# Three tiles per width transform, a smaller first weight load and a shorter warm-up memset in a fused spectral and GELU kernel

**Chip, cores, metric.** One NeuronCore of one Trainium2 chip. The metric is device microseconds of one execution. An execution's time is about 2.1 us more than the span that its trace covers.

## What is computed

The reference adds three terms for an input x of 2048 rows and 640 columns (bf16):

```
xn  = layernorm(x)                                # per row
A   = irfft2(rfft2(xn) * (w_r + 1j*w_i))          # 2-D transform over 2048 x 640, filter, back
B   = gelu(xn @ w1 + b1) @ w2 + b2               # w1: 640 x 1536, w2: 1536 x 640
out = x + A + B
```

Both transforms are written as matrix products with small tables of cosines and sines. A "tile" below is one of the 16 groups of 128 rows.

## The kernel before

The kernel is a list of operations, each with an engine, a priority and an estimate of its length. A list scheduler in the file orders them per engine and sets the semaphores. So any setting (priorities, zones of PSUM banks, which tiles are staged) acts through the resulting order. PSUM is the memory that TensorE writes its products to. TensorE's work in order of time: a warm-up on constants; products with W1 (128 columns for tiles 0 and 1, then 256 and 512), into which transposes and the transforms are woven; products with W2; final products.

The settings, the loads of the head and the warm-up:

```python
STAGED = (0, 2, 4, 6, 8, 10)      # tiles whose W2 product is finished early and parked in SBUF
LAG = 4                           # by how many tiles VectorE's folding trails its normalisation
WARM = 10
...
load_x(0, 1)
...                               # identity, b1
load_x(1, 1)
load_w1(0)                        # each part: three chunks of 128 columns, 480 KB
load_w1(1)
load_w1(2)
load_x(2, 2)                      # tiles 2 and 3
load_w1(3)
...
K.op([("dve", 0.3)], 200, ... e.memset(gT[:, 0, 0:640], 0.5), writes=[B_wm])
warm = K.op([("pe", WARM * 0.43)], 200, mms(lambda: [(ps(B_wp.slot, 0, 512),
            gT[:, 0, 0:128], gT[:, 0, 128:640], True, True)] * WARM), ...)
```

The width transform of two tiles, once along D before the filter (table `etab`) and once after it (`getab`). 640 columns are folded to four sums of 160 terms; of these, 128 rows are the main product, and the remaining 32 rows of all four sums run side by side on four strips of 32 rows:

```python
def five(bufs, main, rem, tab):
    lst = []
    for n, part in ((0, 0), (0, 1), (1, 1), (1, 0)):      # tile, main (0) or remainder (1)
        for g in range(4):
            o_ = ps(bufs[g // 2].slot + g % 2, Q4 * n, Q4 * n + Q4)
            if part == 0:
                lst.append((o_, main(g, n), tab[:, Q4 * g:Q4 * g + Q4], n == 0, n == 1))
            else:
                lst.append((o_, rem(g, n), tab[32 * g:32 * g + 32, 4 * Q4:5 * Q4], n == 1, n == 0))
    return lst
```

The order main 0, remainder 0, remainder 1, main 1 means that TensorE leaves the 128-row form once per pair of tiles. I call that an excursion. Eight pairs along D and eight after the filter make 16.

Of the kernel before, what the change touches and what calls it, by code (L numbers as in the profile page):

```python
# [8 lines left out]
F32 = dt.float32  # L9
# [4 lines left out]
D = 640  # L14
F = 1536
H2 = 320
# [98 lines left out]
ZONE = {'hps': ((2, 8), (0, 4), (2, 8), (2, 8), (0, 4), (4, 8), (2, 8)), 'bps': (0, 4), 'cps': (0, 8), 'dps': (0, 4), 'eps': (0, 6), 'fps': (2, 8), 'fst': (0, 8), 'yps': (0, 8), 'tps': (2, 6), 'aps': (0, 8)}  # L115
PRIO = {'hps': 41.9, 'gelu': 211.2, 'pb': 57.3, 'pc': 141.2, 'filt': 203.4, 'ipc': 358.6, 'xb': 326.2, 'eps': 56.7, 'fin': 29.1, 'fst': 17.0}
BLOCKS = ((0, 1), (1, 2), (2, 4), (4, 6), (6, 8), (8, 12), (12, 16))
AHEAD = 3
STAGED = (0, 2, 4, 6, 8, 10)
XRAT = 4  # L120
LAG = 4
WARM = 10
DEPTH = 5
PACE = 5
BYDMA = (6, 7, 8, 9, 10, 11, 12, 13, 14, 15)

# [266 lines left out]
def bass_parallel_sum__spectral_gfnet__dense_activation_gelu__prompt_kernel(  # L393
# [21 lines left out]
    with ExitStack() as es:  # L415
# [23 lines left out]
        W1 = sb("W1", [128, 4, 5, 384])  # L439
# [5 lines left out]
        xb4 = sb("Xb", [128, 2, 4 * KP])  # L445
# [5 lines left out]
        xot = sb("xo", [128, 5, D], F32)  # L451
# [6 lines left out]
        YO, Y2, YF = 0, 6 * D, 10 * D  # L458
# [9 lines left out]
        p_xn, p_x1, p_xf, p_xb, p_y, p_t, p_z, p_zs = Pool(4), Pool(2), Pool(2), Pool(2), Pool(2), Pool(2), Pool(2), Pool(2)  # L468
        p_yo, p_y2, p_yf, p_xo, p_os = Pool(3), Pool(2), Pool(3), Pool(5), Pool(4)
# [23 lines left out]
        K.op([("pool", 0.1)], 99, lambda e, _: e.memset(view(xb4, KP - 2, [[2 * KP, 4], [1, 3]]), 0.0), writes=[B_xbpad])  # L493
        K.op([("pool", 0.1)], 99, lambda e, _: e.memset(view(xb4, 2 * KP - 1, [[2 * KP, 4], [1, 1]]), 0.0), writes=[B_xbpad])
# [5 lines left out]
        B_w1s = [Buf(f"w1_{j}") for j in range(4)]  # L500
# [8 lines left out]
        def load_w1(j):  # L509
            load(W1[:, j, :, :], w1v[:, :, 384 * j:384 * j + 384], B_w1s[j], 491520, rate=340e3)  # L510
# [36 lines left out]
        K.op([("dve", 0.3)], 200, lambda e, _: e.memset(gT[:, 0, 0:640], 0.5), writes=[B_wm])  # L547
        warm = K.op([("pe", WARM * 0.43)], 200, mms(lambda: [(ps(B_wp.slot, 0, 512), gT[:, 0, 0:128], gT[:, 0, 128:640], True, True)] * WARM), reads=[B_wm], writes=[B_wp])

# [98 lines left out]
        for blk, (c0, c1) in enumerate(BLOCKS):  # L648
            s0, s1 = 128 * c0, 128 * c1
            for fc in range(NFC):  # L650
                hps = Buf(f"hps{blk}_{fc}", psum, 1, ZONE["hps"][min(blk, len(ZONE["hps"]) - 1)])
                B_gT[blk, fc] = Buf(f"gT{blk}_{fc}")
                pr = PRIO["hps"] - blk - fc / 20
                part = []
                for js in ((0, 1, 2), (3, 4)):
                    part = [K.op([("pe", len(js) * mm_us(s1 - s0))], pr + 0.01 * len(part), mms(lambda s0=s0, s1=s1, fc=fc, hps=hps, js=js: [
                        (ps(hps.slot, 0, s1 - s0), W1[:, fc // 3, j, 128 * (fc % 3):128 * (fc % 3) + 128], xnT[:, j, s0:s1], j == 0, j == 4) for j in js]),
                        reads=[B_w1s[fc // 3]] + B_xnT[c0:c1], writes=[hps], gate=part)]
                hps_ops.setdefault(blk, []).append(part[0])
                K.op([("act", act_us(s1 - s0, 1))], pr + PRIO["gelu"], lambda e, _, s0=s0, s1=s1, fc=fc, hps=hps: e.activation(  # L660
                    gT[:, fc, s0:s1], ps(hps.slot, 0, s1 - s0), ACT.Gelu_apprx_tanh, bias=b1col[:, fc:fc + 1], scale=1.0),
                    reads=[hps, B_b1c], writes=[B_gT[blk, fc]], after=())
# [3 lines left out]
        def five(bufs, main, rem, tab):  # L666


            lst = []
            for n, part in ((0, 0), (0, 1), (1, 1), (1, 0)):  # L670
                for g in range(4):
                    o_ = ps(bufs[g // 2].slot + g % 2, Q4 * n, Q4 * n + Q4)
                    if part == 0:
                        lst.append((o_, main(g, n), tab[:, Q4 * g:Q4 * g + Q4], n == 0, n == 1))
                    else:
                        lst.append((o_, rem(g, n), tab[32 * g:32 * g + 32, 4 * Q4:5 * Q4], n == 1, n == 0))
            return lst

        def two(buf):
            return PS[buf.slot // 2][:, :].rearrange("p (b n) -> p b n", b=2)[:, :, 0:2 * Q4].rearrange("p b (n k) -> p n b k", n=2)  # L680
        IPC = 0.78
        FIVE = 1.0
        pb_ops, filt_ops, cps_ops, t_ops = [], [], {}, {}
        B_v = [Buf(f"v{q}") for q in range(16)]
        for pair in range(8):
            Y, TB, Z, xb = Buf(f"Y{pair}", p_y), Buf(f"T{pair}", p_t), Buf(f"Z{pair}", p_z), Buf(f"xb{pair}", p_xb)
            bps = [Buf(f"bps{pair}_{v}", psum, 2, ZONE["bps"]) for v in range(2)]
            pb_ops.append(K.op([("pe", FIVE)], PRIO["pb"] - pair / 5, mms(lambda pair=pair, bps=bps: five(
                bps, lambda g, n: Xa[:, g, 2 * pair + n, :], lambda g, n: Xa[32 * g:32 * g + 32, 4, 2 * pair + n, :], etab)),
                reads=B_xa + [B_e], writes=bps, gate=cps_ops.get(pair - 2, [])))  # L690
            for v in range(2):
                K.op([("dve", dve_us(640)), ("act", act_us(640))], PRIO["pb"] - pair / 5,
                     copy(lambda v=v, xb=xb: view(xb4, xb.slot * 4 * KP + v * (KP + 1), [[2 * KP, 2], [1, 2], [2, Q4]]),
                          lambda v=v, bps=bps: two(bps[v])), reads=[bps[v]], writes=[xb])
            cps = [Buf(f"cps{pair}_{r}", psum, 2, ZONE["cps"]) for r in range(2)]
            cps_ops[pair] = [K.op([("pe", 0.78)], PRIO["pc"] - pair / 5, mms(lambda pair=pair, cps=cps, xb=xb: [
                (ps(cps[r].slot + hi, 0, KP)[64 * qq:64 * qq + 64], mtab[64 * hi:64 * hi + 64, 1 if pair == qq == 0 else 0, v, r, :],
                 xb4[64 * hi:64 * hi + 64, xb.slot, (2 * qq + v) * KP:(2 * qq + v + 1) * KP], v == 0, v == 1)
                for r in range(2) for v in range(2) for hi in range(2) for qq in range(2)]), reads=[xb, B_xbpad, B_m], writes=cps, gate=t_ops.get(pair - 2, []))]
# [66 lines left out]
        B_w2s = [Buf(f"w2_{i}") for i in range(4)]  # L766
        for i in range(4):
            load(W2[:, 3 * i:3 * i + 3, :], w2v[:, 3 * i:3 * i + 3, :], B_w2s[i], 491520, after=[o for blk in hps_ops for o in hps_ops[blk][3 * i:3 * i + 3]])
# [14 lines left out]
        def second(c, pcs, fps, gate, done):  # L783

            part = list(gate)
            for f0 in range(0, NFC, 2):
# [3 lines left out]
                    reads=B_w2s[f0 // 3:(f0 + 1) // 3 + 1] + [B_gT[block_of[c], fc] for fc in range(f0, f0 + 2)], writes=[fps], gate=part)]  # L790
# [9 lines left out]
        for cp in range(8):  # L800
            yo, y2, yf = Buf(f"yo{cp}", p_yo), Buf(f"y2{cp}", p_y2), Buf(f"yf{cp}", p_yf)
            pr = PRIO["eps"] - cp / 5
            eps_ = [Buf(f"eps{cp}_{v}", psum, 2, ZONE["eps"]) for v in range(2)]
            K.op([("pe", FIVE)], pr, mms(lambda cp=cp, eps_=eps_: five(
                eps_, lambda g, n: V[:, (0, 2, 3, 1)[g], 2 * cp + n, :], lambda g, n: V[32 * g:32 * g + 32, 4, 2 * cp + n, :], getab)),
                reads=B_v + [B_ge], writes=eps_, gate=[fin_ops[2 * cp - 5]] if cp > 2 else [])
            for v in range(2):
                K.op([("act", act_us(640)), ("dve", dve_us(640))], pr,
                     copy(lambda v=v, yo=yo: view(Wf, YO + yo.slot * 2 * D + H2 * v, [[D, 2], [Q4, 2], [1, Q4]]),
                          lambda v=v, eps_=eps_: two(eps_[v])), reads=[eps_[v]], writes=[yo], after=filt_ops)  # L810
            for k, op in enumerate((ALU.add, ALU.subtract)):
                K.op([("dve", dve_us(D, 2))], pr + 2, lambda e, _, k=k, op=op, yo=yo, y2=y2: e.tensor_tensor(  # L812
                    out=view(Wf, Y2 + y2.slot * 2 * D + (H2 - 1) * k, [[H2, 4], [1 - 2 * k, Q4]]),
                    in0=view(Wf, YO + yo.slot * 2 * D, [[H2, 4], [1, Q4]]), in1=view(Wf, YO + yo.slot * 2 * D + Q4, [[H2, 4], [1, Q4]]), op=op),
                    port=True, reads=[yo], writes=[y2])
            for k, op in enumerate((ALU.add, ALU.subtract)):
                K.op([("dve", dve_us(D, 2))], pr + 3, lambda e, _, k=k, op=op, y2=y2, yf=yf: e.tensor_tensor(
                    out=view(Wf, YF + yf.slot * 2 * D + (D - 1) * k, [[D, 2], [1 - 2 * k, H2]]),
                    in0=view(Wf, Y2 + y2.slot * 2 * D, [[D, 2], [1, H2]]), in1=view(Wf, Y2 + y2.slot * 2 * D + H2, [[D, 2], [1, H2]]), op=op),
                    port=True, reads=[y2], writes=[yf])  # L820
            for n in range(2):
                c = 2 * cp + n
# [10 lines left out]
                for pcs in (WHOLE,) if c < 15 else (((0, 0, H2),), ((0, H2, H2 + Q4),), ((0, H2 + Q4, D),)):  # L833
                    a, b = pcs[0][1], pcs[-1][2]
                    os_, fps = Buf(f"os{c}_{a}", p_os), Buf(f"fps{c}_{a}", psum, len(pcs), ZONE["yps" if c in STAGED else "fps"])
                    if c not in STAGED:
                        part = second(c, pcs, fps, part + fin_gate(c), False)
                    fin_ops[c] = K.op([("pe", sum(mm_us(hi - lo) for _, lo, hi in pcs))], PRIO["fin"] + 1 - c / 10, mms(lambda c=c, n=n, pcs=pcs, yf=yf, fps=fps: [
                        (ps(fps.slot + k, 0, hi - lo), htab[:, c, :], view(Wf, YF + yf.slot * 2 * D + D * n + lo, [[1, hi - lo]]), c in STAGED, True) for k, lo, hi in pcs]),
# [38 lines left out]
```

## Time and profile before

| | before |
|---|---|
| time, median of the first three executions | 154.83 us (154.74 to 154.84) |
| span of the profiled execution | 154.2 us |
| time of that same execution | 156.34 us |
| TensorE busy | 149.2 us, 97% |

The lines of the profile are shown and read in the prediction. Two hints for reading them: a timeline row is a merged run of equal instructions, so the distance from the start of one row to the start of the next is what the engine spent; the length of a matmul (219 to 380 ns) is its latency, not its cost: 128-column products of 219 ns start every 56 ns at full clock.

### The profile page before, as it was taken

The page shows a single profiled execution, that of the slowest core. Times are in us where ns is not written, and L with a number is a line of the kernel's source. Part 1 is how long each engine was busy: PE and PEld are TensorE (multiplying, and loading weights), DVE is VectorE, ACT ScalarE, POOL GpSimd, SP SyncE. Part 2 cuts the span into 40 slices and gives each one's busy share as a digit, 9 for nine tenths or more (in the row PEclk, how much of TensorE's full clock was granted, in tenths as well). Part 3 has the DMA queues.
Part 4 walks back from the last instruction along what each step waited for, and adds up shares of the span by engine and source line. Part 5 has one row for each costly group of instructions (what it writes and reads, how often), then busy time and mean ns, then how long its engine had stood idle before and what let it go on. Part 6 is the DMA issues. An engine that isn't in the chain of part 4 may idle for free.

```text
span 154.2 us, 3759 instructions
## 1 busy us (share of the span) xinstructions
PE 149.2 (97%) x1546; PEld 103.4 (67%) x1546; DVE 117.1 (76%) x267; ACT 86.8 (56%) x176; POOL 21.0 (14%) x33
## 2 busy tenths in 40 slices
PE   5899999999999999999999999999999999999993
PEld 2399888899665536445556766766777777777773
DVE  3859699999994799499499769768977988862222
ACT  3169978998796697878877536873303333210000
POOL 1201120111200000000000022493022221020000
PEclk9999999999999999999999999999999999999999
DMA  4999934869989300134214043199956346541111
GB/s 115 314 367 397 267 100 91 248 139 121 166 168 201 116 0 0 17 115 132 59 70 132 0 89 76 31 222 253 228 128 168 98 123 173 129 128 47 45 71 56
DMA packets 20792, 20.81 MB, mean 135 GB/s; under 512 B 8360, under 2 KB 17448, under 8 KB 20648
## 3 DMA queue, kind: packets, MB, share of 16 engines
q1 hardware_dynamic: 18304, 15.30, 38.1%
q0 software_dynamic: 2304, 5.24, 15.1%
q8 instruction: 12, 0.20, 0.5%
q10 hardware_dynamic: 168, 0.04, 0.1%
q14 instruction: 4, 0.03, 0.1%
HBM read 13.69 MB, written 2.62 MB: 106 GB/s over the span
## 4 chain that ended last, share of the span: by engine, by line
PE 92%; DMA 4%; ACT 1%; DVE 1%; SPq 1%; issue 0%
PE ps L477 91%; DMA W<-in_B_w_dram 4%; PE ps L602 1%; ACT Xb L484 1%; SPq L472 1%; DVE xnT L487 0%; DVE ost L842 0%
## 5 line engine op out<-in xcount | busy, mean ns | idle before, releaser
L477 PE MATMUL ps<-xnT,W 128*128 128x256 bf16 (+2 forms) x420 | 58.2, 294 | 0.9 <-DMA W<-in_B_w_dram 0.6
L477 PE MATMUL ps<-W,gT 128*128 128x320 bf16 (+1 forms) x396 | 56.5, 295 | 0.0
L477 PEld LDWEIGHTS ps<-W,gT 128*128 128x128 bf16 x396 | 37.4, 98 | 14.3 <-issue 0.8
L477 PEld LDWEIGHTS ps<-xnT,W 128*128 128x128 bf16 x420 | 36.1, 101 | 14.3 <-issue 1.3
L660 ACT ACTIVATE gT<-ps,b1col 128x256 bf16<-128x256 f32 (+2 forms) x84 | 40.3, 506 | 8.8 <-PE ps L477 6.2
L842 DVE TENSOR_TENSOR ost<-ps,xo 128x640 bf16<-128x640 f32 (+2 forms) x12 | 8.6, 713 | 12.4 <-PE ps L477 12.4
L829 ACT ACTIVATE xo<-b2bc 128x640 f32<-128x640 bf16 x10 | 7.1, 731 | 19.1 <-DVE ost L842 19.1
L574 DVE BATCH_NORM_STATS2 stats<-XV 128x6 f32<-128x320 bf16 x32 | 14.1, 469 | 2.1 <-DMA XV<-in_A_x_dram 2.0
L831 POOL DMA_DIRECT2D xnT<-in_A_x_dram x6 | 5.4, 900 | 61.1 <-DVE xnT L798 61.1
L716 DVE TENSOR_TENSOR T<-Y,Wf 128x1288 bf16<-128x1288 bf16 x16 | 12.6, 829 | 0.8 <-ACT Y L484 0.2
L831 POOL DMA_DIRECT2D xo<-in_A_x_dram x10 | 9.5, 1043 | 18.7 <-ACT xo L829 18.7
L582 POOL TENSOR_TENSOR rstd<-ve,mhalf 128x2 f32<-128x2 f32 (+1 forms) x9 | 6.3, 703 | 34.7 <-DVE ve L581 34.7
L484 ACT ACTIVATE Xb<-ps 128x640 bf16<-128x640 f32 x9 | 7.9, 895 | 3.7 <-PE ps L477 3.7
L487 DVE CAST Y<-ps 128x644 bf16<-128x644 f32 x8 | 6.6, 828 | 4.3 <-PE ps L477 4.1
L484 ACT ACTIVATE XV<-ps 128x640 bf16<-128x640 f32 x11 | 7.4, 700 | 4.0 <-PE ps L477 3.9
L484 ACT ACTIVATE Wf<-ps 128x640 bf16<-128x640 f32 x10 | 6.7, 694 | 4.0 <-PE ps L477 4.0
L477 PE MATMUL ps<-etab,XW 128*128 128x160 bf16 (+1 forms) x128 | 8.6, 233 | 0.0
L477 PE MATMUL ps<-getab,XV 128*128 128x160 bf16 (+1 forms) x128 | 8.6, 233 | 0.0
L812 DVE TENSOR_TENSOR Wf<-Wf 128x640 bf16<-128x640 bf16 x16 | 7.1, 485 | 1.3 <-ACT Wf L484 1.3
L477 PEld LDWEIGHTS ps<-etab,XW 128*128 128x128 bf16 (+1 forms) x128 | 5.5, 95 | 3.8 <-DVE Y L487 0.7
L487 DVE CAST Xb<-ps 128x640 bf16<-128x640 f32 x7 | 6.2, 885 | 2.2 <-PE ps L477 2.2
L484 ACT ACTIVATE XW<-ps 128x640 bf16<-128x640 f32 x11 | 7.4, 700 | 0.5 <-PE ps L477 0.5
(49 smaller groups left out, 146.4 us busy)
## 6 DMA issues: line engine op xcount, KB each, us to landing
W<-in_B_w_dram SPq DMA_DIRECT2D x8, 480.0 KB, 4.7
xo<-in_A_x_dram POOLq DMA_DIRECT2D x10, 320.0 KB, 4.9
out_dram<-ost SPq DMA_DIRECT2D x15, 160.0 KB, 2.3
XV<-in_A_x_dram SPq DMA_DIRECT2D x7, 320.0 KB, 8.0
xnT<-in_A_x_dram POOLq DMA_DIRECT2D x6, 320.0 KB, 4.6
Wf<-in_A_w_r_dram SPq DMA_DIRECT2D x7, 160.5 KB, 4.8
Wf<-in_A_w_i_dram SPq DMA_DIRECT2D x7, 160.5 KB, 3.8
gtab<-c_G SPq DMA_DIRECT2D x1, 512.0 KB, 7.3
```

The costliest lines, as they stand in the source:

```text
L472: return K.op([(eng, cost)], 0, lambda e, _: e.dma_start(dst, src), reads=reads, writes=[buf], after=after, nbytes=nbytes, rate=rate)
L477: ins = e.matmul(o_, lhsT=lw, rhs=rh, start=st, stop=sp_)
L484: return e.activation(dst(), src(), ACT.Copy, scale=scale)
L487: return e.tensor_copy(dst(), src())
L574: K.op([("dve", 0.4)], 100 - c, lambda e, _, c=c, h=h: e.bn_stats(stats[:, c, 6 * h:6 * h + 6], view(XV, c * D + H2 * h, [[1, H2]])), read ...
L582: K.op([("pool", 0.75)], 100 - c, lambda e, _, a=a, b=b: e.tensor_tensor(out=rstd[:, a:b], in0=ve[:, a:b], in1=mhalf[:, 0:b - a], op=ALU.pow),
L660: K.op([("act", act_us(s1 - s0, 1))], pr + PRIO["gelu"], lambda e, _, s0=s0, s1=s1, fc=fc, hps=hps: e.activation(gT[:, fc, s0:s1], ps(hps. ...
L716: t_ops[pair].append(K.op([("dve", 0.05 + dve_us(4 * KP, 2))], pr, lambda e, _, k=k, Y=Y, TB=TB, pair=pair: e.tensor_tensor(out=view(TT, T ...
L812: K.op([("dve", dve_us(D, 2))], pr + 2, lambda e, _, k=k, op=op, yo=yo, y2=y2: e.tensor_tensor(out=view(Wf, Y2 + y2.slot * 2 * D + (H2 - 1 ...
L829: K.op([("act", act_us(640))], 30, lambda e, _, xov=xov: e.activation(xov(0, D), b2bc[:], ACT.Copy), reads=[B_b2b], writes=[xi], gate=[z_l ...
L831: K.op([("pool", 1.2)], 50, lambda e, _, c=c, xov=xov: e.dma_start(xov(0, D), xv[:, c, :], accum_op=ALU.add), reads=[xi], writes=[xo], nby ...
L842: os_ops.append(K.op([("dve", dve_us(b - a))], 95, lambda e, _, a=a, b=b, xov=xov, fps=fps, os_=os_: e.tensor_tensor(out=ost[:, os_.slot, ...
```

## The change

The intent is to lose less of TensorE's time: fewer excursions, an earlier first product, and a warm-up that starts sooner. The core of the diff:

```diff
-STAGED = (0, 2, 4, 6, 8, 10)
-LAG = 4
-WARM = 10
+STAGED = (0, 2, 4, 7, 9)
+LAG = 6
+WARM = 11
+PARTS = (0, 2, 5, 8, 12)
+BPS = {0: (0, 3), 1: (3, 3), 3: (6, 2), 4: (8, 2), 5: (10, 2), 6: (12, 2), 7: (14, 2)}
+EPS = (0, 2, 5, 8, 11, 14, 16)
 ...                              (new numbers in ZONE and PRIO)
-        K.op([("dve", 0.3)], 200, lambda e, _: e.memset(gT[:, 0, 0:640], 0.5), writes=[B_wm])
-        warm = ... gT[:, 0, 0:128], gT[:, 0, 128:640], True, True)] * WARM), ...
+        K.op([("dve", 0.15)], 200, lambda e, _: e.memset(gT[:, 0, 0:128], 0.5), writes=[B_wm])
+        warm = ... gT[:, 0, 0:128], view(gT, 0, [[0, 4], [1, 128]]), True, True)] * WARM), ...
 ...                              (W1 and W2 loaded in the parts that PARTS gives)
-        def five(bufs, main, rem, tab):
+        def five(bufs, main, rem, tab, m):
             lst = []
-            for n, part in ((0, 0), (0, 1), (1, 1), (1, 0)):
-                for g in range(4):
-                    ...
+            head = range((m + 1) // 2)
+            for part, ns in ((0, head), (1, range(m)), (0, range(len(head), m))):
+                for n in ns:
+                    for g in range(4):
+                        ...
+                        lst.append([o_, lw, rh, len(lst) < 4, False])     # start: first product of a bank only
+            for q in lst[-4:]:
+                q[4] = True
             return lst
 ...                              (copies and additions of three tiles at once; buffers sized for three)
```

All remainder products of a group, for two or three tiles, stand together, and `start` is set on the first product of each bank alone. There are now 7 groups along D and 6 after the filter.

## The prediction

> **What bounds the kernel now.** I read the page's busy shares first, then the chain that ended last, then the waits of TensorE alone, then the timeline. The page of the kernel before:
>
> ```profile
> PE 149.2 (97%) x1546; PEld 103.4 (67%) x1546; DVE 117.1 (76%) x267; ACT 86.8 (56%) x176; POOL 21.0 (14%) x33
> ...
> PE 92%; DMA 4%; ACT 1%; DVE 1%; SPq 1%; issue 0%
> ```
>
> TensorE is busy for 149.2 of 154.2 us and carries 92% of the chain; no other engine passes 76%. A busy matmul row is not yet work at full rate, so the second question is where TensorE stood still. The view of waits, filtered to TensorE, has only three rows:
>
> ```profile
> PE ps L477 <- DVE gT L547: 1.6, 1, 1.6
> PE ps L477 <- DMA W<-in_B_w_dram: 0.6, 1, 0.6
> PE ps L477 <- DVE xnT L487: 0.3, 1, 0.3
> ```
>
> That is 2.5 us: 1.6 before the warm-up, 0.6 for the first part of W1, 0.3 for the transposed tiles 2 and 3. The other 2.4 us lie after the last matmul (last addition and last store). So a gain can come only from the head (before 17.6 us), from TensorE work that is taken away, or from slots that TensorE wastes inside its "busy" time. I measured the last by start-to-start distances. Timeline of TensorE around one width transform (group "five"), and near the end, where 160-column products run alone:
>
> ```profile
> 65.76 1.07 PE L477 MATMUL ps<-etab,XW 128*128 128x160 bf16 x16
> 66.67 0.38 PE L477 MATMUL ps<-xnT,W 128*128 128x512 bf16 x1
> ...
> 149.84 0.99 PE L477 MATMUL ps<-W,gT 128*128 128x160 bf16 x12
> 150.68 0.23 PE L477 MATMUL ps<-Wf,htab 128*128 128x160 bf16 x1
> ```
>
> Twelve 160-column matmuls take 150.68 - 149.84 = 0.84 us, 70 ns each. A group of two tiles has 8 such products on 128 rows and 8 on 32 rows, of which four run at once: 10 slots of 70 ns = 0.70 us. It takes 66.67 - 65.76 = 0.91 us. The missing 0.21 us sit in two places of the trace: the step from 128-row to 32-row matmuls has 165 ns from start to start (+96), the step back 160 ns (+91) and the one after it 80 ns (+11), together 0.198 us. All 16 groups show it.
>
> The head matters too. TensorE rows between 7.4 and 10.8 us, then between 11 and 16 us:
>
> ```profile
> L477 PE MATMUL ps<-xnT,W 128*128 128x128 bf16 x28 | 3.3, 309 | 0.6 <-DMA W<-in_B_w_dram 0.6
> ```
>
> ```profile
> L477 PE MATMUL ps<-xnT,W 128*128 128x128 bf16 x93 | 5.4, 220 | 0.0
> ```
>
> The same product falls from 309 to 220 ns, and from 107 to 56 ns start to start; the step is at 10.9 us. The page's clock row shows 9 in every slice and hides this, so the first 3.5 us of real work ran at half rate in spite of ten warm-up matmuls (1.59 to 5.84 us).
>
> **What the Trainium skill says.** "TensorEngine Tiling (Array Packing)", Key Properties: a change of tiling mode (not merely of the tile) drains TensorE. The trace agrees: +96 ns in, +102 ns out, nothing between tiles of the same mode (3 to 4 ns). "TensorE: Matmul & The Clock Gate", Back-to-back issue gap: about N/2.4 + 2.5 ns warm, 69 ns for N = 160; measured 69 to 70. The same page, Part 1: the array starts at half clock and goes to full clock after a busy window of about 3.4 us, and the window is free-running. The trace agrees with half rate at first; it puts the step at 10.9 us, so window edges one and two steps earlier would lie near 7.5 and 4.1 us (an estimate from that page's window). From 4.1 to 7.5 TensorE stood idle for 0.6 us, from 0.7 to 4.1 for 0.9 us; neither window sufficed. "PSUM — Partial Sum Buffer", The four PSUM rules: first_mm clears a whole bank's bits, and later groups in that bank may start without it if their columns are disjoint. This is what the new "five" relies on (start only on the first product of each bank); it is about right results, not time.
>
> **The change part by part.**
>
> 1. Width transforms by three tiles. The along-D groups go from 8 to 7 (3, 3, 2, 2, 2, 2, 2), the inverse ones from 8 to 6 (2, 3, 3, 3, 3, 2). A group has one excursion to 32 rows whether it holds two tiles or three, because all remainder products are put together; matmul count and columns stay. 16 - 13 = 3 excursions x 0.198 = **-0.59 us**, directly on TensorE's path. VectorE's fold additions fall from 32 to 24, wider ones, and the copies out of PSUM from 32 to 26; both engines are off the path.
>
> 2. First part of W1 with two chunks instead of three. The old equal parts of 480 KB landed at 7.26, 8.75 and 10.23 us, 1.48 us apart; a third less gives about 0.5 us, 6.8 us (estimate). But the first matmul also needs tile 0 transposed, and ScalarE's copy of it ended at 6.70 + 0.38 = 7.08 us. So the first real matmul goes from 7.40 to about 7.2: **-0.2 us**. Before tiles 2 and 3 the queue now has 8 chunks, not 9, so they land about 0.5 us earlier than 11.1. In the old trace TensorE ended its 128-column work at 17.15 and waited until 17.62 for that chain (0.47 us lost). I take **-0.3 us**.
>
> 3. Warm-up. The memset shrinks from 640 columns (0.59 us) to 128, about 0.2 us by its rate, so the warm-up starts near 1.2 instead of 1.59; eleven matmuls of 427 ns then end at 5.9, where the ten ended at 5.84. By itself this moves no real work. It is worth something only if the longer busy stretch brings the full clock one window earlier. In the likely 0.7-4.1 window the busy share goes from 73% to about 85%. If the clock then steps up before 7.5 us, the 33 intervals between 7.4 and 10.9 save 51 ns each, 1.7 us; the arrival of W1's parts and tiles 2 and 3 would eat a part, and I count **-1.2 us** if it happens, with a chance of 0.35.
>
> 4. Priorities, PSUM zones, five tiles staged instead of six, W2 in new parts. TensorE's matmul count does not change. Old filler: when the first inverse group started (101.95 us), 40 of the 144 staged matmuls were left (5.4 us), and the first final product came 4.0 us later. With 120 staged, 16 would be left, plus two unstaged tiles in the two remaining slots (48 matmuls, 6.5 us). Enough, so I put 0, with a bias of +0.1 us for new waits for PSUM banks.
>
> Sum without the clock: -0.59 - 0.2 - 0.3 + 0.1 = -1.0, **153.8 us**. With it: **152.6 us**. Weighted 0.65 and 0.35: 153.4 us.
>
> **The rivals.**
>
> (a) A wait replaces the removed ones. A three-tile group holds four banks for 1.25 us of products and then a copy of 960 columns (ScalarE took 0.70 us for 640), and the final tiles have only two double slots where they had three. If TensorE runs dry between the filter and the inverse transform, or waits for banks, half a microsecond to one is lost: 154.3 to 155. For it: the one stall of the middle that I can see, at 93.3 us (0.26 us over the normal distance), is such a wait. Against it: TensorE is busy 19.9 of every 20 us between 40 and 140.
>
> (b) The head is hidden anyway. At 17.1 us TensorE waits for a chain of x loads, VectorE statistics and transposes; if VectorE sets it (tiles 2 and 3 were normalised by 15.0, and their transposes then stood behind 58 matmuls until 16.04), a quicker start gives only a longer wait there. Then only the 0.59 of part 1 and about 0.2 remain: 154.1.
>
> (c) The clock steps up early and everything behind it follows: 152 to 152.6. For it: the change touches just this. Against it: no run here shows which busy share suffices, and the three timed runs of before agree within 0.1 us, so the step seems to lie at a stable place.
>
> (d) VectorE becomes the bound: it was 100% busy from 24 to 40 us, but TensorE had filler and lost nothing; the change takes work off it. Unlikely.
>
> **Range and chances.** The sure part is 0.59 us; the head gives 0 to 2, new waits take 0 to 1. That is 152.3 to 154.8 for 8 in 10. Faster by over 2% needs 151.7, that is the clock case in full plus everything else: 0.04. Slower by over 2% needs 157.9, a stall of over 4 us that nothing announces: 0.01. Within 2%: 0.95.
>
> **What would show it right or wrong.** Step 1: 13 excursions, groups of three taking about 12 x 70 + 3 x 70 + 200 = 1.25 us start to start, still +96 and +102 at the edges. Step 2: first real matmul near 7.2 us, released by ScalarE's or VectorE's copy and not by W1; shorter wait at 17 us. Step 3: distances of 107 ns until about 10.9 us, or 56 ns from about 7.5 or before. Step 4: no TensorE wait over 0.3 us between 40 and 150 us, and a tail after the last matmul still of 2.4 us. I am wrong if the full clock comes later than before, if excursions got costlier with three tiles, or if waits of more than a microsecond stand before the first final products.

## The result

The changed kernel took 153.25 us (median of four executions, 153.09 to 153.88); the kernel before took 154.79 us beside it. A ratio here is the mean time of one kernel's executions over that of the other's in the same rounds, so it is not quite the ratio of the medians: 0.991, 95% interval 0.9881 to 0.9938. Executions over 1.5% slower than the fastest of the same kernel are left out of the means. The interval leaves out 1, so a gain of about 1% is clear of the scatter. The results are correct.

The page of the changed kernel, busy shares and chain:

```profile
PE 147.4 (97%) x1547; PEld 101.9 (67%) x1547; DVE 115.7 (77%) x255; ACT 83.9 (55%) x174; POOL 20.8 (14%) x33
...
PE 92%; DMA 4%; SPq 1%; issue 0%; DVE 0%
```

TensorE is still the bound, with the same shares. Its waits:

```profile
PE ps L480 <- DVE gT L556: 1.1, 1, 1.1
PE ps L480 <- ACT xnT L487: 0.4, 1, 0.4
```

The wait before the warm-up is 0.5 us shorter, the wait for W1 is replaced by one for the copy of tile 0, and the wait for tiles 2 and 3 is gone. Timeline of TensorE at the first real products, then at the first width transform of three tiles and behind it:

```profile
6.98 0.62 PE L480 MATMUL ps<-xnT,W 128*128 128x128 bf16 x8 [0.37 <-ACT xnT L487]
```

```profile
46.75 1.43 PE L480 MATMUL ps<-etab,XW 128*128 128x160 bf16 x24
48.02 1.67 PE L480 MATMUL ps<-xnT,W 128*128 128x512 bf16 x7
```

A group of three takes 48.02 - 46.75 = 1.27 us. Its 12 + 3 slots of 70 ns are 1.05 us, so one excursion, about 0.2 us, is left, as before. And the early matmuls, from 7 to 10.8 us:

```profile
L480 PE MATMUL ps<-xnT,W 128*128 128x128 bf16 x59 | 3.8, 220 | 0.4 <-ACT xnT L487 0.4
```

They run at full clock (220 ns) where the profile of before had 309 ns.

For comparing traces I cut each into three: the **head** up to the first 256-column matmul, the **stretch** from there to the start of the last matmul, and the **tail** behind it. The tail is 2.59 or 2.60 us in every trace. I read the starts from the timeline. The experiments ran in three jobs, each on another chip and each with 11 executions of the kernel before; the changed kernel itself ran beside them only in the last (a_again).

| trace (of the experiments below) | first real product | end of head | stretch |
|---|---|---|---|
| before, profile of the prediction | 7.40 | 17.62 | 133.95 |
| before, again (b_again) | 7.73 | 16.61 | 133.95 |
| before, new warm-up (b_warm) | 7.22 | 16.12 | 134.02 |
| before, twice the excursions (b_twice) | 7.51 | 17.59 | 137.72 |
| changed | 6.98 | 15.51 | 133.14 |
| changed, again (a_again) | 6.80 | 15.57 | 133.07 |
| changed, old warm-up (a_warm) | 6.90 | 15.74 | 133.13 |
| changed, one warm-up matmul (a_cold) | 7.07 | 16.33 | 133.06 |
| changed, equal W1 parts (a_wide) | 7.12 | 15.97 | 133.07 |
| changed, six excursions more (a_cut) | 7.16 | 15.73 | 134.30 |
| changed, groups of two (a_groups) | 6.85 | 15.18 | 134.55 |
| changed, LAG = 4 (a_lag) | 6.91 | 15.64 | 135.23 |
| changed, six groups along D (a_six) | 7.06 | 16.14 | 134.39 |
| the same with LAG = 7 (a_six7) | 6.84 | 15.68 | 133.31 |

The stretch repeats within 0.08 us for the same order of instructions, so it resolves what the times, which scatter by about 1 us, do not. The head does not repeat like that: in the eight traces with the new parts of W1 and a full warm-up, TensorE's order is the same up to 21 us or beyond, and yet the head ends anywhere from 15.18 to 16.14 us. So a head of one trace shows a difference of half a microsecond only if the times agree.

### The profile page after: what moved, and what is told of

It is laid out like the page before. It is cut to its first block, busy times and chain, and to the rows that moved or that the text cites. A ratio compares the mean times of both kernels' runs of the same rounds, so it can differ in the third digit from the quotient of the medians.

```text
span 151.2 us, 3740 instructions
## 1 busy us (share of the span) xinstructions
PE 147.4 (97%) x1547; PEld 101.9 (67%) x1547; DVE 115.7 (77%) x255; ACT 83.9 (55%) x174; POOL 20.8 (14%) x33
## 4 chain that ended last, share of the span: by engine, by line
PE 92%; DMA 4%; SPq 1%; issue 0%; DVE 0%
PE ps L480 92%; DMA W<-in_B_w_dram 4%; SPq L475 1%; PE ps L611 1%; DVE ost L866 0%
## 5 line engine op out<-in xcount | busy, mean ns | idle before, releaser
L480 PE MATMUL ps<-xnT,W 128*128 128x256 bf16 (+2 forms) x420 | 57.3, 288 | 0.5 <-ACT xnT L487 0.4
L480 PEld LDWEIGHTS ps<-xnT,W 128*128 128x128 bf16 x420 | 34.9, 98 | 14.2 <-issue 1.3
L669 ACT ACTIVATE gT<-ps,b1col 128x256 bf16<-128x256 f32 (+2 forms) x84 | 39.2, 506 | 4.5 <-PE ps L480 2.8
L487 ACT ACTIVATE Xb<-ps 128x640 bf16<-128x640 f32 (+1 forms) x7 | 7.0, 999 | 5.1 <-PE ps L480 5.0
L487 ACT ACTIVATE Wf<-ps 128x960 bf16<-128x960 f32 (+1 forms) x6 | 5.3, 875 | 7.1 <-PE ps L480 7.1
L487 ACT ACTIVATE XV<-ps 128x640 bf16<-128x640 f32 x9 | 6.2, 699 | 4.0 <-PE ps L480 4.0
L490 DVE CAST Xb<-ps 128x640 bf16<-128x640 f32 (+1 forms) x7 | 6.9, 988 | 1.9 <-PE ps L480 1.9
L487 ACT ACTIVATE Zs<-Z 128x128 bf16<-128x128 bf16 (+1 forms) x31 | 6.1, 266 | 3.5 <-DVE Z L744 3.4
L490 DVE CAST Wf<-ps 128x960 bf16<-128x960 f32 (+1 forms) x6 | 6.3, 1044 | 2.3 <-PE ps L480 2.3
L490 DVE CAST XV<-ps 128x640 bf16<-128x640 f32 x7 | 5.7, 821 | 2.7 <-PE ps L480 2.7
```

What stands on the lines that cost most here:

```text
L480: ins = e.matmul(o_, lhsT=lw, rhs=rh, start=st, stop=sp_)
L487: return e.activation(dst(), src(), ACT.Copy, scale=scale)
L490: return e.tensor_copy(dst(), src())
L669: K.op([("act", act_us(s1 - s0, 1))], pr + PRIO["gelu"], lambda e, _, s0=s0, s1=s1, fc=fc, hps=hps: e.activation(gT[:, fc, s0:s1], ps(hps. ...
```

## The experiments

**Was the late clock a property of the kernel?** b_again is the kernel before, unchanged.

> The kernel before, unchanged, timed against itself. Theory A (the clock's step falls at a different place in different executions): the profile that I predicted from is of an execution with a late step (10.9 us after the start), while the timed executions had it earlier, because the profiled execution lasted 156.34 us and the timed ones 154.8. Then a fresh trace should show full clock from about 5 to 8 us and a span of about 152.7 us, with the same work from 20 us on. Theory B (the step is always late in this kernel, and the profile merely adds time): span 154.2 again and step at about 10.9 us. In both, the ratio is 1.000 within 0.003.

Measured: 155.18 us against 155.08 us, ratio 0.9992 (0.9949 to 1.0036); span 153.2 us. TensorE between 7.4 and 10.8 us, and at the end of the head:

```profile
L478 PE MATMUL ps<-xnT,W 128*128 128x128 bf16 x46 | 3.1, 219 | 1.2 <-DMA W<-in_B_w_dram 1.1
```

```profile
16.61 0.83 PE L478 MATMUL ps<-xnT,W 128*128 128x256 bf16 x6 [0.32 <-DVE xnT L488]
```

The same products run at 219 ns and at full clock; the head ends 1.0 us earlier than in the profile that I predicted from, although W1 landed 0.3 us later, and the stretch is the same to 0.01 us. So theory A holds (the step was late in that execution, not in the kernel): the first profile was of an execution in which the clock stepped up late. Of the 11 executions of before in this job, two took 156.72 and 156.77 us, the others 154.45 to 155.64 us.

**The warm-up.** b_warm puts the new warm-up alone into the kernel before; a_warm puts the old one back into the changed kernel. The order on every engine stays.

```diff
-  e.memset(gT[:, 0, 0:640], 0.5)     ... gT[:, 0, 128:640] ... * WARM          # 10
+  e.memset(gT[:, 0, 0:128], 0.5)     ... view(gT, 0, [[0, 4], [1, 128]]) ... * (WARM + 1)
```

> The kernel before with the new warm-up alone (memset of 128 columns, eleven matmuls), everything else in the same order. If the gain of the change were mainly the earlier clock (rival c), this alone should win 1 to 1.5 us (ratio 0.991 to 0.993). If the timed executions of before already have an early step (theory A), it gives 0 to 0.3 us (ratio 0.998 to 1.000), and warm-up starts at about 1.1 us in the trace.

> The changed kernel with the old warm-up (memset of 640 columns, ten matmuls), everything else in the same order. Main theory: part 3 is worth little, so 153.2 to 153.5 us (ratio to before 0.990 to 0.992). Rival c (the clock is the main gain): back to 154.3 or more (ratio 0.997 or more), with the clock's step later in the trace.

Measured: b_warm 154.96 us against 155.08 us, ratio 0.9996 (0.9945 to 1.0046); a_warm 153.44 us, ratio to before 0.9888 (0.9847 to 0.9928). The warm-up began at 1.06 us with the short memset and at 1.59 us with the long one, and the medians moved by 0.1 us (b_warm to before) and 0.1 to 0.2 us (a_warm to the changed kernel in the other jobs), within the scatter. Rival (c), which asked for 1 us or more, falls.

There may be something in the rare executions. With the old warm-up 6 of 56 executions in all jobs lay more than 1.6 us above the fastest of their kernel in their job; with the new one 0 of 52, though the largest excess there is 1.57 us. The two of those six that were traced (the first profile, and b_twice's) both show the step at 10.8 to 10.9 us. That would fit a warm-up that prevents late steps. But I chose the limit after seeing the times, and all six are executions of the old order (before and b_twice), while a_warm, which has the old warm-up in the new order, had none in six, and neither had b_warm. So the order may be the reason as well as the warm-up; it is not settled.

**What the warm-up is worth at all.** a_cold has one warm-up matmul in place of eleven, in the same order.

```diff
-  ... True, True)] * WARM)
+  ... True, True)] * 1)
```

> The changed kernel with one warm-up matmul instead of eleven, same order. The real work then starts at half clock in every execution, and the step comes one window of busy work later, 10 to 14 us. Theory (the warm-up as such is worth a late step): 1.2 to 2.2 us more than the changed kernel, with a wide scatter between executions; the stretch behind the first 256-column matmul unchanged at 133.1 us unless the step falls into it. Rival (the head is bound by loads and VectorE, half clock is hidden): under 0.5 us more.

Measured: 154.11 us, ratio 0.9942 (0.9894 to 0.9989), 0.8 us over the changed kernel of the same job (153.31 us). That is between the two expectations; no execution of the one was as fast as any of the other (153.88 us at least, against 153.73 at most). TensorE's timeline:

```profile
5.88 0.71 PE L611 MATMUL ps<-ident,T 128*128 128x128 bf16 x5 [4.21 <-DVE ve L590]
6.52 0.19 PE L565 MATMUL ps<-ident,b1t 12*128 12x12 bf16 x1
7.07 1.03 PE L480 MATMUL ps<-xnT,W 128*128 128x128 bf16 x8 [0.36 <-ACT xnT L487]
```

After 4.2 us of idling the first eight products took 1.03 us instead of 0.62, and the step came at 9.5 us, 2.5 us after the first product and 3.7 us after the first transpose. The head ended 0.77 us later than a_again's, and the stretch was unchanged. So half clock in the head cost about 0.8 us on the path here; it was not hidden.

**What an excursion costs.** b_twice reorders the products inside each group of the kernel before, so that TensorE goes to 32 rows twice per pair.

```diff
-            for n, part in ((0, 0), (0, 1), (1, 1), (1, 0)):
+            for n, part in ((0, 0), (0, 1), (1, 0), (1, 1)):
```

(The start and stop flags were set to match.)

> The kernel before with the four products of each group reordered so that each width transform of two tiles goes to 32 rows twice instead of once; same instructions, same order otherwise. Excursions go from 16 to 32. If one costs 0.198 us on the path, time rises by 16 x 0.198 = 3.2 us (ratio 1.020 to 1.021). If the excursions were hidden by other waits (rival), the rise is under 1 us.

Measured: 157.85 us against 155.08 us, ratio 1.0171 (1.0126 to 1.0216). The profiled execution was slow (late step), so I read its stretch alone: 3.77 us longer. Of that, 0.56 us is one wait that before does not have, for VectorE's folding at 42.7 us; the other 3.2 us are 16 excursions of 0.20 us. The wait stands ahead of the first width transform, so the reordering did not make it; it belongs to this execution, and the fast ones were not traced. In the times the rise is 2.8 us, somewhat less than 3.2; the mean of before in that ratio also includes one execution of 156.72 us.

a_cut does the same to the six three-tile groups of the changed kernel, in an unchanged order:

```diff
-  for part, ns in ((0, head), (1, range(m)), (0, range(len(head), m))):
+  for part, ns in (... as before ...) if m < 3 else ((0, (0,)), (1, (0,)), (0, (1,)), (1, (1, 2)), (0, (2,))):
```

> The changed kernel in the same order, but each of its six three-tile groups goes to 32 rows twice instead of once (19 excursions instead of 13). Main theory (an excursion costs 0.198 us on the path): 6 x 0.198 = 1.2 us more than the changed kernel, so about 154.5 us, ratio to before about 0.996 to 0.999; the stretch from the first 256-column matmul to the last matmul goes from 133.14 to 134.3 us in the trace. Rival (the gain lay in fewer, wider copies and additions, not in excursions): unchanged, 153.2 us.

Measured: 154.48 us, ratio to before 0.996 (0.993 to 0.999), so 1.2 us more than the changed kernel's 153.25 us (in another job); the stretch is 134.30 us. The first group of it:

```profile
46.98 1.65 PE L480 MATMUL ps<-etab,XW 128*128 128x160 bf16 x24
48.46 1.46 PE L480 MATMUL ps<-xnT,W 128*128 128x512 bf16 x6
```

From start to start 1.48 us instead of 1.27. (134.30 - 133.14) / 6 = 0.19 us per excursion, on the path. The rival that this part of the gain lay in wider copies is out: those are untouched here.

**Groups of two in the changed kernel.** a_groups sets the groups back; the scheduler orders anew.

```diff
-BPS = {0: (0, 3), 1: (3, 3), 3: (6, 2), ...}     EPS = (0, 2, 5, 8, 11, 14, 16)
+BPS = {p: (2 * p, 2) for p in range(8)}          EPS = tuple(range(0, 17, 2))
```

> The changed kernel with groups of two tiles throughout (16 excursions), all else as changed; the scheduler orders anew. Main theory: 0.6 us more than the changed kernel, 153.7 to 154.0 us, and the stretch from the first 256-column matmul to the last at about 133.7 us. Rival (three tiles at a time carries most of the 1.5 us gain): 154.5 us or more. Rival (grouping hidden): 153.2 us.

Measured: 154.6 us, ratio to before 0.9978 (0.9945 to 1.0011); stretch 134.55 us, 1.41 us more than the changed kernel's. My expectation was 0.6, and the time alone would fit the first rival. Three excursions are 0.6 us of it. By start-to-start distances this order also has 0.7 us more of waits in the stretch, the largest 0.38 us at 79.3 us. So taking the groups out of a tuned order shows their own cost plus that of an order nobody tuned. a_cut, with its unchanged order, is the clean measure.

**The first part of W1.** a_wide brings W1 in four equal parts while each product waits for the part number that it waited for, so that the order of TensorE, VectorE, ScalarE and GpSimd is the same.

```diff
-            a, n = PARTS[j], PARTS[j + 1] - PARTS[j]
+            a, n = WIDE[j], WIDE[j + 1] - WIDE[j]          # WIDE = (0, 3, 6, 9, 12)
```

> The changed kernel in the same order, but W1 arrives in four equal parts of three chunks (each product still waits for the part it waited for). Tiles 2 and 3 of x then queue behind 9 chunks, not 8. Main theory (the head gains from the smaller first part and the earlier x tiles): 0.4 to 0.8 us more than the changed kernel, first real matmul at 7.3 to 7.7 us released by the load of W1 instead of 6.9 to 7.0, and the first 256-column matmul at 16.0 to 16.4 instead of 15.5 us. Rival (the head's gain comes from the new order of VectorE's work alone): within 0.2 us of the changed kernel.

Measured: 153.86 us, ratio to before 0.9925 (0.99 to 0.9951), 0.4 to 0.6 us more than the changed order in the other jobs (a_warm, a_again, result). Its timeline:

```profile
7.12 0.61 PE L480 MATMUL ps<-xnT,W 128*128 128x128 bf16 x8 [0.67 <-DVE T L602]
...
8.49 6.13 PE L480 MATMUL ps<-xnT,W 128*128 128x128 bf16 x103 [0.38 <-DMA W<-in_B_w_dram]
```

The first part landed at 6.99 us (6.13 in the changed kernel), the second at 8.45 (7.44), and x tiles 2 and 3 at 10.79 (10.21). The first product moved by only 0.14 us, since tile 0 is not ready much sooner; the larger loss is the wait of 0.38 us for the second part. The head ends 0.46 us later and the stretch is unchanged.

This one trace does not show the cost, though. Its head ends within the 15.18 to 16.14 us of the eight traces with the new parts, and four of those also wait for W1: a_warm and a_six7 0.2 us for the second part, a_again 0.2 us and a_six, below, 0.6 us for the third:

```profile
PE ps L480 <- DMA W<-in_B_w_dram: 0.6, 1, 0.6
```

The times speak for a cost: 153.55 to 154.05 us here, against 152.92 to 153.88 us in the 16 executions of the changed order (result, a_again, a_warm), but those ran in other jobs. So a cost of about half a microsecond is likely, not shown, and which part of W1 TensorE waits for differs between executions.

**LAG.** a_lag sets `LAG = 4` in the changed kernel and lets the scheduler order anew.

> The changed kernel with the old setting LAG = 4 (VectorE folds a tile two tiles sooner, ahead of later tiles' normalisation); the scheduler orders anew. Theory S (the part of the gain that neither excursions nor the W1 part explain, about 0.3 us, comes from the order that the settings give): 0.3 to 1.5 us more than the changed kernel, with waits of TensorE that the changed kernel lacks. Rival (settings do nothing by themselves): within 0.2 us of it.

Measured: 155.42 us against 155.47 us, ratio 1.0006 (0.9955 to 1.0057). The whole gain is gone, more than the 0.3 to 1.5 us that I expected. The head is as good as ever (15.64 us); the stretch has two new waits:

```profile
39.07 1.25 PE L480 MATMUL ps<-xnT,W 128*128 128x512 bf16 x5 [0.82 <-DMA xnT<-T]
...
107.50 0.72 PE L480 MATMUL ps<-W,gT 128*128 128x320 bf16 x4 [0.60 <-ACT Wf L487]
```

One is for a tile that a DMA transposes, the other for a copy out of PSUM. This does not make LAG the source of the gain, since the kernel before has LAG = 4 and no such waits. It shows that the savings exist only as long as the order feeds TensorE. The new priorities, by contrast, do nothing on their own: with the old ones the changed kernel's order is the same on all five engines (compared without a run).

**One excursion less again.** a_six uses six groups along D; a_six7 the same with `LAG = 7`, whose order I looked for after a_six had failed. a_again is the changed kernel for comparison.

```diff
-BPS = {0: (0, 3), 1: (3, 3), 3: (6, 2), 4: (8, 2), 5: (10, 2), 6: (12, 2), 7: (14, 2)}
+BPS = {0: (0, 3), 1: (3, 3), 3: (6, 3), 4: (9, 3), 6: (12, 2), 7: (14, 2)}
```

> A version that should beat both: along D six groups (3, 3, 3, 3, 2, 2) instead of seven, 12 excursions. Main theory: 0.2 us less than the changed kernel, about 153.05 us (ratio to before 0.986 to 0.990), if no new wait for a PSUM bank appears; a new wait would make it equal or slower.

> The changed kernel, unchanged, for comparison with the three others on the same chip: 153.2 us (ratio to before 0.988 to 0.992), the stretch from the first 256-column matmul to the last matmul 133.1 us.

> Six groups along D (12 excursions) again, with LAG = 7, which gives another order without the two waits (0.6 us each) that the first such version had at 90 and 106 us. If those waits alone ate the gain: 0.2 us less than the changed kernel, 153.0 us, stretch from the first 256-column matmul to the last of about 132.9 us. If three-tile groups throughout cannot be fed: 153.5 us or more.

Measured: a_six 154.56 us, ratio 0.9975 (0.9943 to 1.0007), a miss. Its timeline has two waits that the changed kernel does not have:

```profile
91.11 1.12 PE L480 MATMUL ps<-W,gT 128*128 128x320 bf16 x7 [0.56 <-DVE xnT L821]
```

```profile
106.87 0.72 PE L480 MATMUL ps<-T,htab 128*128 128x320 bf16 x4 [0.42 <-DVE T L841]
```

The first is for the addition that empties a staged tile's PSUM banks, the second for the folds of the first final tiles; its head also has the wait of 0.6 us for W1 shown above, which is not a matter of the groups. a_again gave 153.31 us, ratio 0.9877 (0.9833 to 0.992), and a_six7 153.4 us, ratio 0.9879 (0.9836 to 0.9923). a_six7 has neither large wait, but two of 0.2 us at 54 and 74 us, and its stretch is 0.2 us longer than the changed kernel's instead of 0.2 shorter. No version beat the changed kernel.

## Why the prediction was right, and where it was not

The time, 153.25 us, lies 0.15 us from the predicted 153.4 and inside the range. That is partly luck: the number was a mixture of two cases, and the argument for one of them was mistaken.

**Step 1, excursions, -0.59 us: right.** 13 are left, and each still costs +96 and +102 ns at its edges in the trace. a_cut (0.19 us each) and b_twice (0.20 us each) show that this lies on the path. Of the stretch's gain of 0.81 us it is three quarters; a further 0.12 us are waits that became shorter, and about 0.1 us I cannot name. This is the part of the gain whose cause is shown.

**Step 2, W1 in smaller parts, -0.2 and -0.3 us: likely right in sum, wrong in the split.** Undoing it costs about 0.5 us in the times, across jobs; the trace alone does not resolve it. The first part landed at 6.13 us, not at the estimated 6.8, but the first product gains little from that (0.14 us in a_wide); the waits for W1 that a_wide and the traces with the new parts show are for the second or third part. The wait at 17 us in the old head was not ended by the earlier x tiles either: a_wide, with late x tiles, does not have it. It went with the new order, in which the transposes of tiles 2 and 3 no longer stand behind all 128-column products.

**Step 3, the clock: the step that failed.** The prediction took the late clock of the profiled execution for a property of the kernel ("the step seems to lie at a stable place") and hung a possible gain of 1.2 us on it. The step of the clock is a property of the execution. The window edges near 4.1 and 7.5 us, estimated from that one step, go with it: in the eleven traces with an early step it came anywhere from 3.7 to 6.8 us. The timed executions of before mostly had it early already, by their times, which could have been read beforehand: the profiled execution took 156.34 us and the timed ones 154.8. The warm-up change moves the median by 0.1 to 0.2 us (b_warm, a_warm), within the scatter. The changed kernel does run its head at full clock, as in the case that I gave a chance of 0.35, but most timed executions of before did so too, so nothing was gained by it.

**Step 4, order and buffers, +0.1 us: wrong sign, small.** The sum without the clock was 153.8 us and the measured time is 0.5 us less. The new order brought waits down rather than up: the wait of 0.17 us at 93 us (the prediction read 0.26, counting the change of row form, 0.09 us, as part of it) and that of 0.5 us at the end of the head are gone, while one of 0.13 us came at 103 us. How much of the head's 1.1 us (b_again to changed) is order stays open: with W1 undone the head still ends 0.15 us before b_warm's and 0.64 us before b_again's, and these two differ by 0.5 us between themselves, as their first products do (7.22 and 7.73 us). On average the two end at 16.4 us and the eight of the new parts at 15.65, so the head's gain is nearer 0.7 us than 1.1 (an estimate from these traces); with the stretch's 0.8 it makes up the 1.5 us in the times. The filler estimate held: no wait over 0.13 us by start-to-start distances stands in the changed kernel's stretch.

**The rivals.** (a), a new wait, did not happen in the changed kernel but did in a_six, a_lag and a_groups, with 0.7 to 2 us each. (b), the hidden head, falls: between the first profile and b_again the head's end moved with the clock by 1.0 us, and a_cold moves it by 0.77 us, in both cases with the times to match. (c) falls, as said. (d) was not seen.

## What to carry to other kernels

On a TensorE-bound kernel, measure cost by the distance from one matmul's start to the next: waste inside "busy" time, like a change of row form, showed there and in no busy share, and what was added or removed of it here went straight into the time as long as the order still fed the engine. Before reading a head from a single profile, compare that execution's time with the timed ones; the clock can make them different executions. Take several traces of a head before reading half a microsecond from it. Undo a part in an unchanged order of instructions, or you measure the order.

## What the Trainium skill lacked or had wrong

- "TensorEngine Tiling (Array Packing)", Key Properties, says that a mode switch drains TensorE but not what it costs. Here: 96 ns into the 32-row form and 102 ns back (91 + 11), 0.198 us per excursion; 92 to 96 ns into the 64-row forms where nothing else is waited for.
- "TensorE: Matmul & The Clock Gate", Back-to-back issue gap, gives sustained spacings in a real kernel of about 81 ns for 128 columns and 131 ns for 512. Here, with a weight load for each matmul, they are 56 and 216 ns, which is that page's other formula, N/2.4 + 2.5 ns.
- The same page, Part 1, calls the window free-running and the cold count run-variable, which fits the traces: with ten or eleven warm-up matmuls the full clock came from 2.7 to 5.7 us after the first of them in eleven traces, and 9.2 to 9.3 us after it in two. It puts the ramp at under 1% of a typical kernel's span and gives no figure for a late step: here the one pair of traces of the same kernel with a late and an early step differs by 1.0 us (spans of 154.2 and 153.2 us), 0.7%.
- The same page, Part 4, says that the full clock does not engage for transposes. Here transposes went from 107 to 56 ns, start to start, when the clock stepped up. Whether they count as activity, these runs cannot tell.
